# Column-wise softmax sums for the last two head blocks of an attention and gated-MLP kernel, with all final additions on VectorE

## Chip, cores, metric

One core of a Trainium2 chip. The metric is the device time of one execution in microseconds (us). "Span" is the time from the first to the last instruction of one profiled execution; it is about 1.8 us shorter than the device time. Engines are named as the profile names them: PE (TensorE matmul), PEld (TensorE weight load), DVE (VectorE), ACT (ScalarE), POOL (GpSimd), SP (SyncE, which issues the transfers).

## The reference, cut to what matters

```python
B, S, D, H = 1, 2048, 512, 32           # head size 16; MLP width F = 1792; all bf16
xn = layernorm(x)
scores = einsum("bhqd,bhkd->bhqk", q, k) * 16 ** -0.5
p = softmax(scores)                      # 32 x 2048 x 2048 exponentials
out = x + (einsum("bhqk,bhkd->bhqd", p, v) merged) @ wo + mlp(xn)
```

The kernel works on blocks of 512 queries by 4 heads: 32 blocks in all. It multiplies the unnormalised exponentials with V and a column of ones (the "PV" matmuls), so that the softmax sum of each head appears as row 16 of that head's 32 partitions. A block is then divided by its sums, and goes into the output projection.

## The kernel before

The kernel is a list of operations, each with an assumed duration. A static list scheduler in Python simulates the engines with these durations and so fixes the order of the instructions on each engine; each engine then works through its list in that order, waiting on semaphores: in the profile below PE stands 2.65 us at one matmul while others queue behind it.

For 30 of the 32 blocks the division goes through DRAM and POOL, far from the critical path. The last two blocks have no time for this. They spread each sum over its 32 partitions by a matmul with a column of an identity, take the reciprocal of the whole spread tile on DVE, and multiply:

```python
# last-but-one block (one piece of 512 columns); ps_b bank 1 holds the spread sums
def sums(e):
    for j in range(4):                   # 4 heads, 32 partitions each, fp32
        ins = e.matmul(ps_b[32*j:32*j+32, 1, :], ident32[:, 32*j+DH:32*j+DH+1].to_broadcast([128, 32]),
                       o_sb[:, to.slot, :], start=True, stop=True, tile_position=(0, 32*j))
    return ins
G.op("PE", 920, sums, mode="col", ...)
G.op("DVE", 680, lambda e: e.reciprocal(rb[:, tr.slot, :], ps_b[:, 1, :]), ...)     # 680 ns is assumed
G.op("DVE", 610, lambda e: e.tensor_tensor(oT_of(tn), rb[:, tr.slot, :], o_sb[:, to.slot, :], ALU.mult), ...)
# last block: the same in two halves of 256 columns, reciprocal assumed at 400 ns each   [cut]

# final rows: 4 blocks of 128 rows; groups 2, 4, 5 of the projection are still to be added
for i in range(4):
    if i in FIN_PE:                      # FIN_PE = (1,): the residual enters PSUM by 4 fp32 identity matmuls
        for k in range(4):
            G.op("PE", 225, ... e.matmul(bank_of(tz)[:, 128*k:128*k+128], ident32[:], resid(i)[...], start=(k == 0), stop=False) ...)
    for g, pr in ((2, NU-10), (4, NU-9), (5, NU+10)):
        G.op("PE", 216, fn, ...)         # 4 column tiles of the projection; g=4: last-but-one block, g=5: last block
    if i not in FIN_PE:
        G.op("DVE", 610, ... e.tensor_tensor(xn_sb[...], bank_of(tz), resid(i), ALU.add) ...)
    else:
        G.op("ACT", 600, ... e.activation(xn_sb[...], bank_of(tz), ACTF.Copy) ...)
    dma(... out2[128*m:128*(m+1), :] <- xn_sb ...)    # issued by SP, 128 KB
```

Row block 3 collects its projection in `ps_b` bank 1, the same bank that holds the spread sums of the last-but-one block. So its first projection matmul has to wait until the reciprocal has read that bank.

The softmax here doesn't subtract the row's maximum and nothing guards it: scores larger than these inputs give would overflow.

## Time and profile before

| | before |
|---|---|
| device time, three runs | 790.36, 790.53, 791.13 us |
| span of the profiled execution | 788.1 us, mean granted clock 0.996 |
| ACT / PE / DVE busy | 97% / 96% / 94% |
| end of the last exponential | 776.07 us |
| end of the last addition | 784.66 us |
| end of the last output issue | 785.44 us |

The page's first part: busy time of each engine, share of the span, number of instructions.

```profile
PE 756.7 (96%) x9270; PEld 225.2 (29%) x9270; DVE 740.0 (94%) x1065; ACT 763.3 (97%) x679; POOL 165.0 (21%) x178
```

Over most of the span all three of ACT, PE and DVE are nearly full; ACT, with its exponentials, is the fullest. The end differs. First the timeline of ACT: start, duration, line, operation, and in brackets the idle time before it and what ended it.

```profile
734.10 32.90 ACT L1232 ACTIVATE ring<-ps_sc 128x1024 bf16<-128x1024 f32 x29
770.71 5.36 ACT L1232 ACTIVATE ring<-ps_sc 128x1536 bf16<-128x1536 f32 x5 [3.72 <-PE ps_sc L1164]
782.99 0.60 ACT L1274 ACTIVATE xn_sb<-ps_sc 128x512 bf16<-128x512 f32 x1 [6.92 <-PE ps_sc L1262]
```

ACT starves for 3.72 us before its last five exponentials, because PE has made no scores. DVE's timeline of the same stretch:

```profile
764.82 3.35 DVE L1080 RECIPROCAL rb<-ps_b 128x512 f32<-128x512 f32 x1
768.09 1.16 DVE L1197 TENSOR_TENSOR dring<-dring 128x2048 bf16<-128x2048 bf16 x1
769.16 0.68 DVE L1081 TENSOR_TENSOR x_sb<-rb,Wv 128x512 bf16<-128x512 f32 x1
777.19 0.76 DVE L1061 COPY Wv<-ps_b 128x256 f32<-128x256 f32 x2 [7.34 <-PE ps_b L1140]
778.62 1.76 DVE L1042 RECIPROCAL rb<-ps_b 128x256 f32<-128x256 f32 x1 [0.68 <-PE ps_b L1036]
780.30 1.69 DVE L1042 RECIPROCAL rb<-ps_sc 128x256 f32<-128x256 f32 x1
781.91 0.69 DVE L1047 TENSOR_TENSOR x_sb<-rb,Wv 128x256 bf16<-128x256 f32 x2
782.77 1.29 DVE L1271 TENSOR_TENSOR xn_sb<-ps_sc,xnT 128x512 bf16<-128x512 f32 x2 [0.18 <-PE ps_sc L1262]
783.98 0.68 DVE L1271 TENSOR_TENSOR xn_sb<-ps_b,xnT 128x512 bf16<-128x512 f32 x1
```

(The trace names tiles by the memory they reuse: "Wv" is here the evicted PV block, "x_sb" the normalised one, "xnT" the residual.) The scheduler took the first reciprocal for 0.68 us; it takes 3.35. From the waits, in us: total, times, longest:

```profile
ACT ring L1232 <- PE ps_sc L1164: 3.7, 1, 3.7
PE ps_b L1262 <- DVE rb L1080: 2.6, 1, 2.6
```

PE stood 2.6 us at a final-projection matmul (L1262), and the scores for ACT stood in the queue behind it. PE's timeline and the windows view (stretch, length, busy us and instructions of PE, PEld, DVE, ACT and POOL, granted clock, DMA share, GB/s) show what followed:

```profile
768.23 0.62 PE L1262 MATMUL ps_b<-Wo,x_sb 128*32 128x512 bf16 x4 [2.65 <-DVE rb L1080]
```

```profile
765.00:768.00 3.00, 0.58 (x10) 0.09 (x2) 3.00 (x1) 2.00 (x2) 0.00 (x0) 0.99 0.00 0
768.00:771.00 3.00, 2.77 (x27) 0.66 (x27) 1.85 (x3) 0.29 (x1) 0.00 (x0) 0.50 0.00 0
```

After the stall PE ran on half a clock (0.50; in finer windows from 767.9 to 771.3).

### The profile page before, as it was taken

To read this page: it belongs to the slowest core of one execution; us is meant where nothing else is said; L and a number is where in the kernel's file an instruction comes from. 1 tells how busy PE (TensorE), PEld (TensorE's weight loads), DVE (VectorE), ACT (ScalarE), POOL (GpSimd) and SP (SyncE) were. 2 spreads that over 40 slices of the span, in tenths; PEclk is the share of its full clock that TensorE was granted. 3 is DMA by queue.
4 is the path that set the end of the run, shared out by engine and by line. 5 is a ranking of instruction groups with operands and counts; after the bars stand their busy time and mean duration, and the time that the engine had idled before them with its cause. 6 is when DMAs were issued, how large, how long until landed. Compare 5 with 4: busy or idle time off the path is not lost.

```text
span 788.1 us, 21088 instructions
## 1 busy us (share of the span) xinstructions
PE 756.7 (96%) x9270; PEld 225.2 (29%) x9270; DVE 740.0 (94%) x1065; ACT 763.3 (97%) x679; POOL 165.0 (21%) x178
## 2 busy tenths in 40 slices
PE   8999999999999999999999999999999999999986
PEld 4322222222222222222222223222222222223322
DVE  7689999999999899999999999999999899999994
ACT  6999999999999999999999999999999999999992
POOL 4112131221222113122122112212211212212200
PEclk9999999999999999999999999999999999999998
DMA  7312121212221122211221112221222112332000
GB/s 215 108 47 65 41 70 36 63 48 61 56 70 42 36 62 63 68 46 47 72 56 51 42 49 76 51 66 32 73 55 69 35 53 71 71 82 55 29 15 28
DMA packets 95756, 46.82 MB, mean 59 GB/s; under 512 B 69936, under 2 KB 91824, under 8 KB 95664
## 3 DMA queue, kind: packets, MB, share of 16 engines
q1 hardware_dynamic: 95664, 45.46, 21.3%
q8 instruction: 73, 1.20, 0.6%
q14 instruction: 19, 0.16, 0.1%
HBM read 36.70 MB, written 8.50 MB: 57 GB/s over the span
## 4 chain that ended last, share of the span: by engine, by line
DVE 46%; PE 26%; ACT 26%; issue 1%; DVEq 0%
ACT ring L1232 25%; DVE dring L1180 16%; PE ps_b L697 10%; DVE dring L1196 8%; PE ps_sc L1164 7%; DVE dring L1197 6%; PE ps_b L1140 5%; DVE dring L1192 4%; DVE dring L1194 4%; DVE up_sb L916 3%; DVE hT L920 2%; PE ps_b L1164 2%; DVE Wv L1068 1%; PE ps_b L863 1%; DVE xn_sb L958 1%
## 5 line engine op out<-in xcount | busy, mean ns | idle before, releaser
L1232 ACT ACTIVATE ring<-ps_sc 128x1536 bf16<-128x1536 f32 (+1 forms) x663 | 755.2, 1279 | 6.6 <-PE ps_sc L1164 4.9
L1180 DVE TENSOR_SCALAR dring<-ps_b 128x512 uint16<-128x512 f32 x392 | 269.5, 687 | 19.4 <-PE ps_b L1164 18.8
L1164 PE MATMUL ps_sc<-qm,kT 32*128 32x512 bf16 x1656 | 264.7, 385 | 6.6 <-ACT ring L1232 4.1
L1164 PE MATMUL ps_b<-qm,kT 32*128 32x512 bf16 x392 | 150.1, 383 | 8.8 <-DVE dring L1180 6.3
L1140 PE MATMUL ps_b<-ring,v_aug 128*17 128x512 bf16 x1656 | 152.1, 384 | 0.3 <-DVE Wv L1068 0.2
L1094 POOL TENSOR_TENSOR rrec<-rsum,minus 128x16 f32<-128x16 f32 x30 | 96.3, 3211 | 228.6 <-DMA rsum<-Wv 228.6
L1164 PEld LDWEIGHTS ps_sc<-qm,kT 32*128 32x128 bf16 x1656 | 63.4, 91 | 231.5 <-ACT ring L1232 202.3
L1197 DVE TENSOR_TENSOR dring<-dring 128x2048 bf16<-128x2048 bf16 x98 | 119.5, 1219 | 0.0
L1196 DVE TENSOR_TENSOR dring<-dring 128x2048 f16<-128x2048 bf16 x98 | 119.4, 1219 | 0.0
L1104 POOL TENSOR_TENSOR x_sb<-Wv,rb 128x128 bf16<-128x128 f32 x100 | 46.3, 465 | 285.3 <-DVE dring L1197 77.7
L1192 DVE TENSOR_SCALAR dring<-dring 128x2048 uint16<-128x2048 uint16 x98 | 67.9, 693 | 1.7
L697 PE MATMUL ps_b<-xnT,wus 128*32 128x512 bf16 x896 | 67.9, 384 | 1.1 <-DVE hT L920 0.6
L1194 DVE TENSOR_SCALAR dring<-dring 128x2048 uint16<-128x2048 uint16 x98 | 67.6, 689 | 0.0
L697 PE MATMUL ps_b<-xnT,wgs 128*32 128x512 bf16 x896 | 66.2, 383 | 1.3 <-DVE up_sb L916 1.0
L1140 PE MATMUL ps_b<-dring,vd 128*17 128x512 bf16 x784 | 65.5, 381 | 0.0
L697 PE MATMUL ps_b<-Wd,hT 128*32 128x512 bf16 x768 | 59.8, 383 | 0.1
L1140 PEld LDWEIGHTS ps_b<-ring,v_aug 128*17 128x17 bf16 x1656 | 38.5, 89 | 65.3 <-issue 46.7
L1164 PEld LDWEIGHTS ps_b<-qm,kT 32*128 32x128 bf16 x392 | 35.6, 91 | 66.0 <-DVE dring L1180 52.9
L1140 PE MATMUL ps_b<-dring,v_aug 128*17 128x512 bf16 x392 | 38.6, 384 | 1.5 <-DVE dring L1197 0.7
L1282 PE MATMUL ps_b<-zeros 128*17 128x512 bf16 x456 | 38.9, 382 | 0.0
L916 DVE COPY up_sb<-ps_b 128x512 f32<-128x512 f32 x56 | 38.4, 686 | 0.2 <-PE ps_b L697 0.2
L920 DVE SCALAR_TENSOR_TENSOR hT<-ps_b,up_sb 128x512 bf16<-128x512 f32 x48 | 32.9, 686 | 0.9 <-PE ps_b L697 0.9
(105 smaller groups left out, 363.3 us busy)
## 6 DMA issues: line engine op xcount, KB each, us to landing
rb<-rec_scr SPq DMA_DIRECT2D x30, 256.0 KB
wus<-in_B_W_up_dram SPq DMA_DIRECT2D x56, 128.0 KB, 3.5
wgs<-in_B_W_gate_dram SPq DMA_DIRECT2D x56, 128.0 KB, 2.3
qm<-q_scr SPq DMA_DIRECT2D x30, 128.0 KB
o_scr<-x_sb SPq DMA_DIRECT2D x25, 128.0 KB
q_scr<-qT SPq DMA_DIRECT2D x17, 128.0 KB
xr_sb<-in_A_x_dram SPq DMA_DIRECT2D x16, 128.0 KB, 2.5
out_dram<-xn_sb SPq DMA_DIRECT2D x16, 128.0 KB, 1.8
```

What stands on the lines that cost most here:

```text
L697: ins = e.matmul(bank_of(tile, sub)[32 * j:32 * j + 32, :], st[:, 32 * j:32 * j + 32], mv, start=(i == 0), stop=(i == n - 1), tile_positio ...
L916: G.op("DVE", 610, lambda e: e.tensor_copy(up_sb[:, tup.slot, :], bank_of(tu)), reads=[tu], writes=[tup], prio=slots[1] + EV)
L920: G.op("DVE", 610, lambda e: e.scalar_tensor_tensor(out=h_of(th), in0=bank_of(tg), scalar=0.0, in1=up_sb[:, tup.slot, :], op0=ALU.max, op1 ...
L1094: G.op("POOL", 3000, lambda e: e.tensor_tensor(rrec[:, par, :], rsum[:, par, :], minus[:, 0:1].to_broadcast([128, 16]), ALU.pow), reads=[t ...
L1140: ins = e.matmul(ps_b[32 * j:32 * j + VN, 0, :], v, src[j][1](k), start=(first and k == 0), stop=(last and (k == 2 or not on)), tile_posit ...
L1164: return e.matmul(bank, kT[32 * j:32 * j + 32, gg, 128 * kt:128 * kt + 128], qm[32 * j:32 * j + 32, t_q[(c4, gg)].slot, ee, :], start=True ...
L1180: o = G.op("DVE", 610, lambda e, j=j: e.tensor_scalar(dring[:, tr.slot, 0, 512 * j:512 * j + 512].bitcast(U16), ps_b[:, 2, :], 0.25 * LOG2 ...
L1192: G.op("DVE", 600, lambda e: e.tensor_scalar(b(2, U16), b(0, U16), 0x7F, 0x3F80, op0=ALU.bitwise_and, op1=ALU.bitwise_or), reads=[tr], wri ...
L1194: G.op("DVE", 600, lambda e: e.tensor_scalar(b(1, U16), b(0, U16), 0xFF80, N_MANT, op0=ALU.bitwise_and, op1=ALU.bitwise_or), reads=[tr], w ...
L1196: G.op("DVE", 1140, lambda e: e.tensor_tensor(b(2, FP16), b(2), b(2), ALU.mult), reads=[tm], writes=[tm], prio=u - 3, name="d4", lock=True)
L1197: G.op("DVE", 1140, lambda e: e.tensor_tensor(b(2), b(0), b(2, FP16), ALU.mult), reads=[tm, tr], writes=[tm], prio=u - 3, name="d5", lock= ...
L1232: return e.activation(ring[:, a:a + n, :], ps_sc[:, 3 * k0:3 * k0 + n, :], ACTF.Exp, scale=0.25)
```

## The change

The intent: a reciprocal costs by the column (3.35 us for 512 columns, 1.69 to 1.76 for 256). The sums are only 4 x 512 numbers, so bring them into 16 columns by 128 partitions, invert those, and spread the result afterwards, again with PE. The block is used as the stationary operand and four columns of the identity as the moving one: this transposes just the sum rows. The spread multiplies a broadcast column with the whole identity. Two details come along: row block 1's addition moves from PE and ACT to DVE (`FIN_PE` empty), and the PV matmuls of the last 14 units rather than 5 get early priority. The identity additions' own priority is changed too, which does nothing while `FIN_PE` is empty but matters in e6. The diff is cut; lines after "..." are paraphrased.

```diff
-FIN_PE = (1,)
+FIN_PE = ()
+PV_LAST = 14
+        def spread_sums(src, c0, c1, par, bank_s, bank_r, rd, t_s, t_r, pr, opens=None):
+            def sums(e):
+                for c in range(c0, c1):
+                    ins = e.matmul(bank_s(4 * c, 4 * c + 4), src(128 * c, 128 * c + 128), ident32[:, DH:128:32], start=True, stop=True)
+                return ins
+            o = G.op("PE", 240 * (c1 - c0), sums, mode="full", ...)
+            G.op("DVE", 180, lambda e: e.reciprocal(rrec2[:, par, 4 * c0:4 * c1], bank_s(4 * c0, 4 * c1)), ...)
+            def spread(e):
+                for c in range(c0, c1):
+                    for j in range(4):
+                        ins = e.matmul(bank_r(32 * j, 128 * c), rrec2[:, par, 4 * c + j:4 * c + j + 1].to_broadcast([128, 32]), ident32[:],
+                                       start=True, stop=True, tile_position=(0, 32 * j))
+                return ins
+            G.op("PE", 270 * (c1 - c0), spread, mode="col", ...)
 ... last block, each half h:
-   sums (460) / reciprocal 128x256 (400) / multiply
+   spread_sums(src, 2 * h, 2 * h + 2, ...)
+   t_fin[h].w.append(G.op("DVE", 350, ... ps * src -> oT ...))     # reads the spread from PSUM
 ... last-but-one block:
-   sums (920) / reciprocal 128x512 (680) / multiply
+   spread_sums(lambda a, b: o_sb[:, to.slot, a:b], 0, 4, 0, ..., pr + 80)
+   G.op("DVE", 610, lambda e: e.tensor_tensor(oT_of(tn), ps_b[:, 1, :], o_sb[:, to.slot, :], ALU.mult), ...)
-   prio=u + PV_LAG - (200 if u > NU - 5 else 0)
+   prio=u + PV_LAG - (200 if u > NU - PV_LAST else 0)
 ... identity additions of FIN_PE (row blocks 0 to 2):
-   prio=NU + 2
+   prio=NU - 190
```

More of the change, by code (lines that the diff above doesn't have):

```diff
@@ L483, in bass_parallel_sum__mha_block__glu_gated_reglu__prompt_kernel @@
         rb = sb("rb", [128, 2, 512], FP32)
+        rrec2 = sb("rrec2", [128, 2, 16], FP32)
         rsum = sb("rsum", [128, 2, 16], FP32)
@@ L1021, in bass_parallel_sum__mha_block__glu_gated_reglu__prompt_kernel @@
         t_half, t_fin = [Tile(), Tile()], [Tile(), Tile()]
+        def spread_sums(src, c0, c1, par, bank_s, bank_r, rd, t_s, t_r, pr, opens=None):
+            def sums(e):
+                ins = None
+                for c in range(c0, c1):
+                    ins = e.matmul(bank_s(4 * c, 4 * c + 4), src(128 * c, 128 * c + 128), ident32[:, DH:128:32], start=True, stop=True)
+                return ins
+            o = G.op("PE", 240 * (c1 - c0), sums, mode="full", reads=[rd, t_id32], writes=[t_s], prio=pr - 100, name="sum")
+            if opens is not None:
+                o.opens = ("tail", [o])
+            t_rec = Tile()
+            G.op("DVE", 180, lambda e: e.reciprocal(rrec2[:, par, 4 * c0:4 * c1], bank_s(4 * c0, 4 * c1)), reads=[t_s], writes=[t_rec], prio=pr - 900, name="rec")
+            def spread(e):
+                ins = None
+                for c in range(c0, c1):
[3 more added lines that the diff above has]
+                return ins
+            G.op("PE", 270 * (c1 - c0), spread, mode="col", reads=[t_rec, t_id32], writes=[t_r], prio=pr - 100, name="spread")
+            if opens is not None:
+                G.ops[-1].opens = ()
         def last_normalise(to, pr):
@@ L1025, in src @@
                 return o_sb[:, to.slot, a:b]
-            tn, tr = Tile("oT", P_oT), Tile("rb", P_rb)
-            tt = [Tile("ls", P_b, [2]), Tile("lb", P_sc, [1])]
+            tn = Tile("oT", P_oT)
+            ts = [Tile("ls", P_b, [2]), Tile("lb", P_sc, [1])]
             for h in range(2):
-                def bank(h=h):
-                    return ps_b[:, 2, 256 * h:256 * h + 256] if h == 0 else ps_sc[:, 3, 256 * h:256 * h + 256]
-                def sums(e, h=h, bank=bank):
-                    ins = None
-                    for j in range(4):
-                        ins = e.matmul(bank()[32 * j:32 * j + 32, :], ident32[:, 32 * j + DH:32 * j + DH + 1].to_broadcast([128, 32]),
-                                       src(256 * h, 256 * h + 256), start=True, stop=True, tile_position=(0, 32 * j))
-                    return ins
-                o = G.op("PE", 460, sums, mode="col", reads=[t_half[h], t_id32], writes=[tt[h]], prio=pr - 100, name="sum")
-                o.opens = ("tail", [o]) if h == 0 else ()
-                t_rec = Tile()
-                G.op("DVE", 400, lambda e, h=h, bank=bank: e.reciprocal(rb[:, tr.slot, 256 * h:256 * h + 256], bank()), reads=[tt[h]], writes=[t_rec] + ([tr] if h == 0 else []),
-                     prio=pr - 900, name="rec")
@@ L1044, in last_normalise @@
+                t_r = Tile("lr")
+                spread_sums(src, 2 * h, 2 * h + 2, 1, lambda a, b, h=h: (ps_b[:, 2, :] if h == 0 else ps_sc[:, 3, :])[:, a:b],
+                            lambda p, c, h=h: ps_sc[p:p + 32, 4, c:c + 128] if h else ps_b[p:p + 32, 2, c:c + 128],
+                            t_half[h], ts[h], ts[h] if h == 0 else t_r, pr, opens=True if h == 0 else None)
                 if h:
-                    tr.w.append(G.ops[-1])
-                    G.ops[-1].order.add(tr.w[0])
@@ L1047, in last_normalise @@
-                t_fin[h].w.append(G.op("DVE", 330, lambda e, h=h: e.tensor_tensor(oT_of(tn)[:, 256 * h:256 * h + 256], rb[:, tr.slot, 256 * h:256 * h + 256], src(256 * h, 256 * h + 256), ALU.mult),
-                     reads=[t_rec, t_half[h]], writes=[tn] if h == 0 else [], prio=pr - 900, lock=True))
+                    ts[1].w.append(G.ops[-1])
+                t_fin[h].w.append(G.op("DVE", 350, lambda e, h=h: e.tensor_tensor(oT_of(tn)[:, 256 * h:256 * h + 256],
+                                                                              (ps_sc[:, 4, 256:512] if h else ps_b[:, 2, 0:256]), src(256 * h, 256 * h + 256), ALU.mult),
+                     reads=[ts[h], t_half[h]] + ([t_r] if h else []), writes=[tn] if h == 0 else [], prio=pr - 900))
@@ L1070, in normalise @@
             if (c4, gg, ee) == (NB - 1, NGG - 1, 0):
-                tn, tr, ts, t_rec = Tile("oT", P_oT), Tile("rb", P_rb), Tile("ls", P_b, [1]), Tile()
-                def sums(e):
-                    ins = None
-                    for j in range(4):
-                        ins = e.matmul(ps_b[32 * j:32 * j + 32, 1, :], ident32[:, 32 * j + DH:32 * j + DH + 1].to_broadcast([128, 32]),
-                                       o_sb[:, to.slot, :], start=True, stop=True, tile_position=(0, 32 * j))
-                    return ins
-                G.op("PE", 920, sums, mode="col", reads=[to, t_id32], writes=[ts], prio=pr - 20, name="sum")
-                G.op("DVE", 680, lambda e: e.reciprocal(rb[:, tr.slot, :], ps_b[:, 1, :]), reads=[ts], writes=[tr], prio=pr - 900, name="rec")
-                G.op("DVE", 610, lambda e: e.tensor_tensor(oT_of(tn), rb[:, tr.slot, :], o_sb[:, to.slot, :], ALU.mult),
-                     reads=[tr, to], writes=[tn], prio=pr - 900, lock=True)
+                tn, ts, tr = Tile("oT", P_oT), Tile("ls", P_b, [1]), Tile("lr", P_b, [1])
+                spread_sums(lambda a, b: o_sb[:, to.slot, a:b], 0, 4, 0, lambda a, b: ps_b[:, 1, a:b], lambda p, c: ps_b[p:p + 32, 1, c:c + 128], to, ts, tr, pr + 80)
+                G.op("DVE", 610, lambda e: e.tensor_tensor(oT_of(tn), ps_b[:, 1, :], o_sb[:, to.slot, :], ALU.mult),
+                     reads=[tr, to], writes=[tn], prio=pr - 900)
                 t_oT[(c4, NGG + ee)] = tn
@@ L1142, in pv @@
                     return ins
-                G.op("PE", 225, pv, mode="col", reads=rd, writes=[pv_tile[key]], prio=u + PV_LAG - (200 if u > NU - 5 else 0), name="pv%d" % u,
+                G.op("PE", 225, pv, mode="col", reads=rd, writes=[pv_tile[key]], prio=u + PV_LAG - (200 if u > NU - PV_LAST else 0), name="pv%d" % u,
                      after=u + PV_MIN)
@@ L1254, in bass_parallel_sum__mha_block__glu_gated_reglu__prompt_kernel @@
                     G.op("PE", 225, lambda e, i=i, tz=tz, k=k: e.matmul(bank_of(tz)[:, 128 * k:128 * k + 128], ident32[:], resid(i)[:, 128 * k:128 * k + 128], start=(k == 0), stop=False),
-                         mode="full", reads=[t_id32, t_res[m]], writes=[tz], prio=NU - 20 if i == 3 else NU + 2)
+                         mode="full", reads=[t_id32, t_res[m]], writes=[tz], prio=NU - 20 if i == 3 else NU - 190)
             for g, pr in ((2, NU - 10), (4, NU - 9), (5, NU + 10)):
```

## The prediction

> **What bounds the kernel now.** Over most of the span ScalarE: the page gives ACT 97% busy (exponentials), PE 96%, DVE 94%. The change touches only the last 25 us of 788.1, where two stretches of DVE reciprocal bound it (timeline and chain of waits):
> 1. The last-but-one head pair's RECIPROCAL, 128x512, 3.35 us from 764.82. PE, in order, stands 2.65 us behind it at a final-projection matmul that needs the same bank; no scores are made and ACT sits idle 3.72 us before 770.71. The windows view shows granted clock 0.50 for 768.2 to 770.7. The Trainium skill (TensorE: Matmul & The Clock Gate, Part 1) says that an idle PE is returned to half clock; this trace agrees.
> 2. In the tail, two RECIPROCALs of 128x256 (1.76 and 1.69 us) stand back to back between the sums and the last multiplications. From the end of the last exponential (776.07) to the end of the last addition (784.66) is 8.6 us.
>
> **Cost of the parts.** (3.35-1.72)/256 gives 6.4 ns per column of a reciprocal and about 0.1 us fixed. The Trainium skill (VectorE: DVE Perf Modes, the 8-slice pipeline) speaks of an iterated divide with repeat count 8; the trace shows about 6 cycles at 0.96 GHz, dear by the column anyway. Estimates from it: 16 columns 0.2 us, 8 columns 0.15. So 6.8 us of DVE become about 0.5.
> Added on PE: sums as columns need a full fp32 128x128 weight load each. The identity additions (same stationary size, 128 columns moving) step at 0.42 us; with four moving columns I estimate 0.22, so 0.9 us for the first pair and 0.45 per half. The spread resembles the old sums (512 columns 1.07 us, 256 about 0.6): 1.0 and 0.5 us. Multiplications stay 0.68 and 0.38 us.
> Removed on PE: four identity additions, 1.7 us from 775.6 to 779.3, two ahead of the last PV and one ahead of the last sums (about 0.7 us on the chain). Moved: row block 1's addition from ACT (0.60, parallel) to DVE (0.62 more on the chain).
>
> **On the critical path.** First stretch: the wait for the bank shrinks to what the scheduler assumed, PE doesn't stall or cool, ACT runs on: I expect 3.1 to 3.6 of the 3.72 us idle to go, and the last exponential to end near 772.7. Earlier PV (last 14 units) is worth little by itself.
> Tail, from the last exponential: PV 0.6, eviction 0.45, sums 0.65, reciprocal 0.2, spread 0.65, multiplication 0.4, projection 0.45, four additions 2.5: about 6.0 us against 8.6. Gain 2.3 to 2.6.
> Together 5.4 to 6.2 us of 790.5, 0.7%.
>
> **Predicted:** 784.7 us, 8 in 10 within 782.8 to 787.2. Faster by over 2%: 0.01; within 2%: 0.985; slower by over 2%: 0.005.
>
> **What would show it.** Timeline: RECIPROCALs of 128x16 and twice 128x8, each under 0.25 us; ACT's idle before its last five exponentials under 0.6 us; granted clock near 1.0 up to the last exponential, which ends 772.3 to 773.3; no identity matmuls; four DVE additions in a row, ending about 6 us after it; nothing changed before about 750 us.
>
> **What would make it wrong.** Full-array fp32 sums or 16 small spread matmuls at 2x the estimate, on a PE nearly full there (the chain runs through PE from 740 to 761), so ACT still starves 1 to 2 us; early PV pushing back the last output job, which frees the bank that the sums need; projection matmuls landing between sums and spread in PE's order; a changed order of earlier work; the clock dropping in PE gaps of the tail.

## More of the kernel before

SP's timeline shows the four output issues back to back, 1.95 us, up to 785.44:

```profile
783.49 1.95 SPq L1276 DMA_DIRECT2D out_dram<-xn_sb  x4
```

## The result

The changed kernel took 783.2, 783.4 and 784.0 us, the kernel before in the same rounds 790.21 to 791.13: ratio 0.9911, 95% interval 0.9892 to 0.9931. A ratio here is the mean time of one kernel's fast runs over that of the other's in the same rounds, so not quite the ratio of the medians that are quoted. One more execution, the first and the only profiled one, took 1069.93 us with a granted clock of 0.556 from start to end: a slow state of the chip. It is left aside; none of the later executions of this kernel or its variants showed it, and why that one did is open. The kernel was therefore run once more, unaltered, as the first experiment (783.24 to 783.54 us, five runs; ratio 0.9907, interval 0.9888 to 0.9925). The lines below are from that run.

The page's first part of the kernel after:

```profile
PE 754.2 (97%) x9306; PEld 226.4 (29%) x9306; DVE 734.8 (94%) x1066; ACT 762.5 (98%) x678; POOL 165.7 (21%) x178
```

ACT's timeline now ends with one row of 34 exponentials without a gap, up to 734.29 + 38.06 = 772.35 us, 3.72 us earlier than before:

```profile
734.29 38.06 ACT L1240 ACTIVATE ring<-ps_sc 128x1024 bf16<-128x1024 f32 x34
```

DVE's timeline (all three reciprocals are now L1036):

```profile
764.43 0.25 DVE L1036 RECIPROCAL rrec<-ps_b 128x16 f32<-128x16 f32 x1
764.60 1.16 DVE L1204 TENSOR_TENSOR dring<-dring 128x2048 f16<-128x2048 bf16 x1
772.91 0.76 DVE L1077 COPY Wv<-ps_b 128x256 f32<-128x256 f32 x2 [5.29 <-PE ps_b L1148]
774.03 0.21 DVE L1036 RECIPROCAL rrec<-ps_b 128x8 f32<-128x8 f32 x1 [0.37 <-PE ps_b L1030]
774.48 0.21 DVE L1036 RECIPROCAL rrec<-ps_sc 128x8 f32<-128x8 f32 x1 [0.24 <-PE ps_sc L1030]
775.08 0.42 DVE L1062 TENSOR_TENSOR x_sb<-ps_b,Wv 128x256 bf16<-128x256 f32 x1 [0.40 <-PE ps_b L1042]
776.01 1.89 DVE L1279 TENSOR_TENSOR xn_sb<-ps_sc,xnT 128x512 bf16<-128x512 f32 x3
777.82 0.68 DVE L1279 TENSOR_TENSOR xn_sb<-ps_b,xnT 128x512 bf16<-128x512 f32 x1
```

6.8 us of reciprocal have become 0.67. What PE pays (L1030 are the column sums, L1042 is here the spread) is near the estimates; its timeline for the last-but-one block and for the first half of the last:

```profile
762.64 1.05 PE L1030 MATMUL ps_b<-ident,Wv 128*128 128x4 f32 x8
764.73 1.08 PE L1042 MATMUL ps_b<-ident,rrec 128*32 128x128 f32 x32
773.39 0.61 PE L1030 MATMUL ps_b<-ident,Wv 128*128 128x4 f32 x4
774.37 0.64 PE L1042 MATMUL ps_b<-ident,rrec 128*32 128x128 f32 x16
```

The windows view: no stall, and the clock stays at 1.00.

```profile
765.00:768.00 3.00, 2.93 (x59) 1.12 (x51) 2.58 (x3) 3.00 (x4) 0.00 (x0) 1.00 0.00 0
768.00:771.00 3.00, 3.00 (x45) 0.87 (x45) 0.00 (x0) 3.00 (x4) 0.00 (x0) 1.00 0.00 0
```

SP's timeline: the last output issue ends at 776.73 + 2.12 = 778.85 us.

```profile
776.73 2.12 SPq L1284 DMA_DIRECT2D out_dram<-xn_sb  x4
```

A comparison of the instruction orders in the two traces shows them identical on all engines up to about 760 us. So all that differs lies at the end, and the span can be cut into three pieces: up to the end of the last exponential; from there to the end of the last output issue; and the rest, which is 2.6 to 2.7 us in every one of these profiles (before: 788.1 - 785.44; after: 781.5 - 778.85) and so tells nothing. The two first pieces, from the ACT and SP timelines:

| kernel (profiled run) | last exponential ends | from there to end of last issue | span | clock |
|---|---|---|---|---|
| before | 776.07 | 9.37 | 788.1 | 0.996 |
| after (e0) | 772.35 | 6.50 | 781.5 | 0.999 |
| e1: only the last-but-one block changed | 772.41 | 9.05 | 784.1 | 0.998 |
| e2: only the last block changed | 775.09 | 7.19 | 784.9 | 1.000 |
| e3: only FIN_PE and PV priority | 776.55 | 9.01 | 788.2 | 0.994 |
| e4: before, true durations for the scheduler | 772.27 | 9.60 | 784.5 | 0.997 |
| e5: e1 with a useless wide reciprocal | 776.90 | 9.14 | 788.7 | 0.994 |
| e6: after, FIN_PE back | 772.48 | 6.97 | 782.1 | 1.000 |
| e7: after, PV priority back | 772.87 | 6.66 | 782.2 | 0.999 |
| e8: after, two residuals by bf16 matmul | 772.10 | 6.57 | 781.3 | 1.000 |
| e9: e2 with true duration | 772.09 | 7.42 | 782.2 | 1.000 |
| e10: e8 with two output transfers | 772.36 | 5.75 | 780.8 | 0.999 |
| e11: e8, last transfer issued by ACT | 772.56 | 6.11 | 781.4 | 0.999 |

The gain of 6.6 us of span is 3.7 us of ACT's stall and 2.9 us of tail.

### The profile page after: what moved, and what is told of

It reads as the page before. It is cut to its first block, busy times and chain, and to the rows that moved or that the text cites. A ratio compares the mean times of both kernels' runs of the same rounds, so it can differ in the third digit from the quotient of the medians.

```text
span 1068.1 us, 21160 instructions
## 1 busy us (share of the span) xinstructions
PE 1060.4 (99%) x9306; PEld 249.2 (23%) x9306; DVE 766.3 (72%) x1066; ACT 797.9 (75%) x678; POOL 161.9 (15%) x178
## 4 chain that ended last, share of the span: by engine, by line
PE 98%; DVE 1%; ACT 1%; issue 0%; DVEq 0%
PE ps_b L699 34%; PE ps_b L1148 26%; PE ps_sc L1172 24%; PE ps_b L1172 8%; PE ps_b L1290 4%; PE ps_b L865 1%; ACT ring L1240 0%; PE ps_b L648 0%; PE ps_sc L1270 0%; PE ps_b L1042 0%; PE ps_b L1030 0%; DVE dring L1188 0%; PE ps_sc L648 0%; DVE Wv L1084 0%; PE ps_sc L711 0%
## 5 line engine op out<-in xcount | busy, mean ns | idle before, releaser
L1240 ACT ACTIVATE ring<-ps_sc 128x1536 bf16<-128x1536 f32 (+1 forms) x663 | 789.6, 1235 | 245.9 <-PE ps_sc L1172 146.3
L1172 PE MATMUL ps_sc<-qm,kT 32*128 32x512 bf16 x1656 | 337.8, 481 | 1.1 <-ACT ring L1240 0.6
L1148 PE MATMUL ps_b<-ring,v_aug 128*17 128x512 bf16 x1656 | 211.6, 530 | 0.2
L1172 PE MATMUL ps_b<-qm,kT 32*128 32x512 bf16 x392 | 195.3, 498 | 1.0 <-DVE dring L1188 1.0
L699 PE MATMUL ps_b<-xnT,wus 128*32 128x512 bf16 x896 | 99.3, 543 | 0.1
L699 PE MATMUL ps_b<-xnT,wgs 128*32 128x512 bf16 x896 | 98.3, 550 | 0.1
L1148 PE MATMUL ps_b<-dring,vd 128*17 128x512 bf16 x784 | 97.3, 551 | 0.0
L699 PE MATMUL ps_b<-Wd,hT 128*32 128x512 bf16 x768 | 88.6, 549 | 0.0
L1290 PE MATMUL ps_b<-zeros 128*17 128x512 bf16 x444 | 54.3, 534 | 0.0
L1148 PE MATMUL ps_b<-dring,v_aug 128*17 128x512 bf16 x392 | 53.5, 534 | 0.0
```

Source lines behind the costliest of these rows:

```text
L699: ins = e.matmul(bank_of(tile, sub)[32 * j:32 * j + 32, :], st[:, 32 * j:32 * j + 32], mv, start=(i == 0), stop=(i == n - 1), tile_positio ...
L1148: ins = e.matmul(ps_b[32 * j:32 * j + VN, 0, :], v, src[j][1](k), start=(first and k == 0), stop=(last and (k == 2 or not on)), tile_posit ...
L1172: return e.matmul(bank, kT[32 * j:32 * j + 32, gg, 128 * kt:128 * kt + 128], qm[32 * j:32 * j + 32, t_q[(c4, gg)].slot, ee, :], start=True ...
L1240: return e.activation(ring[:, a:a + n, :], ps_sc[:, 3 * k0:3 * k0 + n, :], ACTF.Exp, scale=0.25)
L1290: ins = e.matmul(ps_b[32 * j:32 * j + VN, 0, :], zeros[:, 0:VN], zmov, start=False, stop=False, tile_position=(0, 32 * j))
```

## The experiments

**Theory:** (1) the 3.35 us reciprocal of the last-but-one block cost time only because PE, in order, stood behind it and starved ACT; (2) the two halves of the last reciprocal lay on the chain of the tail. **Rivals:** the order of PE's work (PV priority, FIN_PE) made the gain; or all of it is in the tail; or DVE's time is itself what counts in the first part, so that only a short reciprocal helps.

Each kernel ran in five rounds (four to six runs) beside the kernel before; e0 to e3, e4 to e7, e8 and e9, e10 and e11 were sent together, each set to one chip but not all to the same one, so medians of different sets are compared with care. All were correct.

### e0: the changed kernel again

> The changed kernel unaltered, once more, because its profiled execution fell in a slow state (clock 0.56 from start to end). Expected in a fast state: 783.0 to 784.3 us, 6.5 to 7.3 us under the kernel before. Theory (stall gone plus shorter tail): ACT's idle before its last five exponentials under 0.6 us, last exponential ends 772.3 to 773.3, last addition 5.5 to 6.2 us after it. Rival (gain is all in the tail): ACT still idles over 2 us there.

783.3 us median, 7.5 under the 790.85 of its rounds, a shade more than the 6.5 to 7.3 expected. ACT's stall is wholly gone, the last exponential ends at 772.35 and the last addition 6.15 us later (778.50). The theory's figures for the trace hold; the rival that expected ACT to idle still falls.

### e1: only the last-but-one block

```diff
 kernel before, with
+ spread_sums(...) for block (3, 3, 0)      # last_normalise, FIN_PE, PV priority as before
```

> The kernel before with only the last-but-one head pair changed (column sums, 16-column reciprocal, spread). Theory: this alone removes the ACT idle of 3.72 us, so 3.2 to 3.9 us faster than before, i.e. about 787.0. Rival 1 (the tail is where all of the gain lies, and the stall is hidden): within 1 us of before. Rival 2 (the order of PE work, PV_LAST, is needed for it): under 2 us gain.

786.13 us median, ratio 0.9943 (0.9928 to 0.9958): 4.5 us faster than before, somewhat above the range of 3.2 to 3.9 set for it. ACT's idle is 0.21 us, and the last exponential ends at 772.41:

```profile
764.05 8.36 ACT L1249 ACTIVATE ring<-ps_sc 128x1024 bf16<-128x1024 f32 x8 [0.21 <-PE ps_sc L1181]
```

The rivals fall: this part alone, without any change of priority, removes the stall.

### e2: only the last block

```diff
 kernel before, with
+ last_normalise of the changed kernel      # last-but-one block, FIN_PE, PV priority as before
```

> The kernel before with only the last head pair changed. Theory: the tail loses two reciprocals of 1.7 us and gains two spreads and fuller sums, 2.4 to 3.2 us faster than before (about 787.7), and the early ACT idle of 3.7 us stays. Rival (the tail hides behind other work): within 1 us of before.

788.34 us median, ratio 0.9966 (0.9948 to 0.9983): 2.7 us faster. The tail is 2.2 us shorter (7.19 against 9.37), and the stall stays, as expected. But its six runs fall into two sorts: 786.72 and 786.94 at a mean clock of 1.000, and 788.0 to 788.99 at 0.996 to 0.997. The profiled run was of the first sort. Its PE, ACT and windows lines:

```profile
768.56 0.40 PE L1277 MATMUL ps_b<-Wo,x_sb 128*32 128x512 bf16 x4 [2.64 <-DVE rb L1095]
```

```profile
769.97 5.12 ACT L1247 ACTIVATE ring<-ps_sc 128x1536 bf16<-128x1536 f32 x5 [2.65 <-PE ps_sc L1179]
```

```profile
768.00:771.00 3.00, 2.44 (x37) 0.79 (x41) 2.17 (x3) 1.03 (x1) 0.00 (x0) 1.00 0.00 0
```

PE stood just as long as in the kernel before (2.64 us against 2.65), in the same order of instructions, but here the clock stayed at 1.00 and ACT lost 2.65 us instead of 3.72. So the 3.72 us are 2.65 of waiting and 1.07 of half clock after it: from the end of its wait to the end of the next scores PE needs 2.44 us in the kernel before and 1.36 here. The same order of instructions and the same stall can go either way. Two more profiled stalls, 2.56 us in e3 and 2.83 us in e5, were followed by half clock too, each time for about 3.4 us; in e3 it set in 0.75 us after PE had resumed. So of four stalls of nearly one length three were followed by it. The Trainium skill (TensorE: Matmul & The Clock Gate, Part 1) says that the activity window runs freely and isn't tied to the kernel's start; two outcomes of one stall agree with that.

The spread of the kernel before fits it: of its 11 runs in these rounds, the three at a mean clock of 0.996 or more took 789.06 to 789.13 us, the eight at 0.992 to 0.994 took 790.17 to 792.58, while the changed kernel, which has no stall, spread over 0.3 us in e0. But the mean doesn't show which outcome a run had. It also counts the half clock after the last matmul (from 785.0 to the end in the profile before), and that profiled run, with half clock after its stall, has a mean of 0.996 and took 789.88 us. Whether the slower runs of e2 and of the kernel before had half clock after the stall is therefore likely and not shown; no trace of them was kept.

### e3: only the priorities

```diff
-FIN_PE = (1,)
+FIN_PE = ()
-... (200 if u > NU - 5 else 0)
+... (200 if u > NU - 14 else 0)
```

> The kernel before with only FIN_PE empty and the PV priority over the last 14 units. Theory: no more than 0.7 us either way, because both reciprocals stay: identity additions off the chain give 0.5 to 0.7 us, the fourth addition on DVE takes 0.6 back. Rival (most of the gain is the reordering): 3 us or more faster.

789.8 us median, ratio 0.9984 (0.9968 to 1.0001): 1.3 us, more than the 0.7 expected, but with an interval that reaches 1. ACT still stalls, in two pieces (2.21 and 1.34 us). The rival "it is the reordering" falls.

### e4: the kernel before with true durations

```diff
-G.op("DVE", 680, lambda e: e.reciprocal(rb[:, tr.slot, :], ...        # last-but-one block
+G.op("DVE", 3280, lambda e: e.reciprocal(rb[:, tr.slot, :], ...
-G.op("DVE", 400, ... e.reciprocal(rb[:, tr.slot, 256*h:256*h+256], ... # last block
+G.op("DVE", 1650, ...
```

> The kernel before with nothing changed but the two durations that its static scheduler assumes for the wide reciprocals (680 to 3280 ns and 400 to 1650 ns, as the trace measures them); the instructions are the same, only PE's order moves. Theory (the 3.7 us of ACT idle came from PE's in-order queue standing at a matmul that waits for the bank): PE now does PV and scores before that matmul, ACT's idle there drops under 1 us, the clock stays near 1.0, 2.5 to 4 us faster than before, about 787. Rival (3.35 us of DVE is itself on the chain, so only a shorter reciprocal helps): within 1 us of before.

786.73 us median, ratio 0.9955 (0.9943 to 0.9968): 3.6 us faster than before. On ACT and DVE the traces show the same instructions in the same order as before; PE's order differs from 765.7 us on. The wide reciprocal is still there, 3.35 us long, and ACT runs through it without a gap:

```profile
765.04 3.35 DVE L1080 RECIPROCAL rb<-ps_b 128x512 f32<-128x512 f32 x1
```

```profile
734.32 37.95 ACT L1232 ACTIVATE ring<-ps_sc 128x1024 bf16<-128x1024 f32 x34
```

The last exponential ends at 772.27, as in the changed kernel. The scheduler, told the truth, put the waiting projection matmul behind PV and two more rounds of scores, and PE waits 0.16 us at it:

```profile
767.67 0.61 PE L1282 MATMUL ps_b<-zeros 128*17 128x512 bf16 x8
768.45 0.40 PE L1262 MATMUL ps_b<-Wo,x_sb 128*32 128x512 bf16 x4 [0.16 <-DVE rb L1080]
```

The first of these lines is a thing not mentioned so far: where the scheduler expects PE to be too idle, it puts in blank matmuls, products with zeros. It placed two groups of four here, and in all one group fewer than before (452 of these matmuls against 456), so the list of instructions isn't quite the same. In the 2.65 us gap of the kernel before there is none. The blanks are not needed for the gain: e1 and the changed kernel have none after 690 us. So DVE's 3.35 us were never on the chain by themselves: the rival falls, and part (1) of the theory is shown.

### e5: a useless wide reciprocal put back

```diff
 e1, with, in front of the 16-column reciprocal
+    e.reciprocal(up_sb[:, 0, :], ps_b[:, 1, :])     # 128x512, result unused; assumed duration unchanged
```

> The version with only the last-but-one pair changed, with a useless 128x512 reciprocal put back on DVE right before the 16-column one; PE's order is the same as in that version. Theory (length of the DVE instruction in front of an in-order PE): PE stalls at the spread for about 3 us and ACT starves again by 2.5 to 4 us, so the gain of 4.5 us mostly goes, 789 to 791 us. Rival (the form of the sums or the bank use made the gain): stays within 1 us of 786.1.

791.17 us median (789 to 791 expected), ratio 1.001 (0.9997 to 1.0022): the whole gain of e1 is gone, and the profile's waits show the stall again, now at the spread (L1044), with ACT's as its consequence:

```profile
ACT ring L1252 <- PE ps_b L1160: 3.6, 1, 3.6
PE ps_b L1044 <- DVE rrec L1037: 2.8, 1, 2.8
```

PE's order is the same as in e1, matmul by matmul in the traces. So neither the form of the sums nor the bank made the gain: an unforeseen 3.35 us in front of an in-order PE makes or unmakes it.

### e6 and e7: one detail of the change undone

```diff
 e6: changed kernel, FIN_PE = (1,)
 e7: changed kernel, PV_LAST = 5
```

> The changed kernel with one part undone: row block 1's residual again added by four identity matmuls on PE and copied out by ACT. Theory: the four matmuls (0.42 us each) land before the last PV and put it back 0.5 to 0.9 us, one addition fewer on DVE gives 0.6 back: within 0.5 us of the changed kernel. Rival (four additions in a row on DVE are what bounds the end): 0.5 us or more faster than the changed kernel.

> The changed kernel with one part undone: early PV only for the last 5 units instead of 14. Theory: within 0.4 us of the changed kernel (783.3). Rival (the earlier PV keeps ACT fed): slower by 1 us or more, with ACT idle in the last 20 us.

e6 took 784.02 us median (ratio 0.9922, 0.991 to 0.9934), e7 783.84 (0.9918, 0.9905 to 0.9932), against 783.3 (0.9907) for the changed kernel in an earlier set of rounds; the intervals overlap, so by the medians the details are worth 0.7 and 0.5 us, a little more than the 0.5 and 0.4 allowed for, and the intervals don't make it sure. The rival of e7 (1 us or more) falls: its last exponential ends 0.52 us later, after 0.22 us of ACT idle at 764.5, and its tail is 0.16 us longer. In e6 the tail is 0.47 us longer, and PE's timeline shows three identity additions ahead of the last PV but one, and one more ahead of the last:

```profile
771.51 0.94 PE L1262 MATMUL ps_sc<-xnT,ident 128*128 128x128 f32 x6
772.38 0.39 PE L1148 MATMUL ps_b<-ring,v_aug 128*17 128x512 bf16 x4
772.70 0.49 PE L1262 MATMUL ps_sc<-xnT,ident 128*128 128x128 f32 x2
773.12 0.39 PE L1148 MATMUL ps_b<-ring,v_aug 128*17 128x512 bf16 x4
```

The last PV starts at 773.12 rather than 772.46. This isn't quite the order of the kernel before, which has two of the four ahead of its last PV: the changed kernel gives them a higher priority (NU - 190 rather than NU + 2), so e6 doesn't undo that one detail alone. From the start of the last PV to the last addition e6 takes 5.54 us against 6.04, so one addition fewer on DVE did give back 0.5 us there; but the last issue ends 6.33 us after it against 6.39, so nearly nothing was left, which the expectation (0.6 us) and its rival both missed. That pointed to another bound on the end.

### e8: two of four additions off DVE

```diff
 changed kernel, with FIN_B = (1, 3):
-            return xnT[:, i, 0:1024].bitcast(FP32)
+            return xnT[:, i, 0:512] if i in FIN_B else xnT[:, i, 0:1024].bitcast(FP32)   # residual kept in bf16
+                if g == 4 and i in FIN_B:                      # one bf16 identity matmul, 128x512
+                    G.op("PE", 225, ... e.matmul(bank_of(tz), ident[:], resid(i), start=False, stop=False) ...)
 blocks 1 and 3 are copied out by ACT
```

> A version meant to beat both: the changed kernel, with the residuals of row blocks 1 and 3 kept as bf16 and added by one bf16 identity matmul each (128x512), so that ACT copies out two of the four blocks beside DVE's two additions. Theory (four additions of 0.62 us in a row on DVE bound the end): last piece ready about 1.0 us earlier, 782.2 to 782.8 us, 0.6 to 1.1 us under the changed kernel. Rival (output issue and landing bound the end, not the additions): within 0.3 us of the changed kernel.

783.52 us median, ratio 0.9918 (0.9904 to 0.9931): no gain. The additions did get done sooner (DVE and ACT both end by 777.30, against 778.50), and yet SP's last issue ends at 776.72 + 1.95 = 778.67:

```profile
776.71 0.59 ACT L1286 ACTIVATE xn_sb<-ps_b 128x512 bf16<-128x512 f32 x1
776.72 1.95 SPq L1288 DMA_DIRECT2D out_dram<-xn_sb  x4
```

My theory of the end falls: SP needs 1.95 us for four issues in a row (344 to 599 ns each), and it can't start before the first block is ready at about 776.7. When the additions are faster, the issues queue; when they are slower, as in the changed kernel, each issue (332 to 400 ns) hides behind the next addition.

### e9: the first part of the change replaced by a true duration

```diff
 e2, with
-G.op("DVE", 680, lambda e: e.reciprocal(rb[:, tr.slot, :], ...
+G.op("DVE", 3280, lambda e: e.reciprocal(rb[:, tr.slot, :], ...
```

> Only the last pair changed, and the last-but-one pair's wide reciprocal kept but told to the scheduler at its true 3280 ns. Theory (the first part of the change is worth only what PE's order is worth): no ACT idle, 783.6 to 784.8 us, within 1.3 us of the changed kernel. Rival (the short first reciprocal has a worth of its own): 786 us or more.

784.37 us median, ratio 0.9928 (0.9915 to 0.994). ACT runs without a gap to 772.09. So the short reciprocal of the last-but-one block buys nothing that a correct number in the schedule would not; what is left to the changed kernel (about 1.1 us by the medians) lies in the tail (7.42 against 6.50), where the identity additions still stand in this version. No run has the wide reciprocal with its true duration and all else as in the changed kernel, so what the identity additions cost there isn't measured alone.

### e10 and e11: fewer issues in SP's row

```diff
 e10: e8, output blocks (0,1) and (2,3) as two transfers of 256 KB
 e11: e8, block 3's transfer issued by ACT after its own copy
```

> The version with two bf16 identity additions (783.5 us), with its four output transfers of 128 KB made two of 256 KB (blocks 0 and 1, blocks 2 and 3). Theory (SyncE's row of four issues of 0.34 to 0.6 us each bounds the end, since the last data were ready at 777.3 but the last issue ended at 778.67): last issue ends at about 777.85, a gain of 0.3 to 0.8 us over that version, 782.7 to 783.2 us. Rival (the 512 KB themselves take that long to move): within 0.2 us of it.

> The same version, with the last output transfer (block 3) issued by ScalarE itself right after it has written the block; SyncE issues the other three. Theory (SyncE's row of issues): last issue ends near 778.05 instead of 778.67, a gain of 0.3 to 0.7 us, 782.8 to 783.2 us. Rival (moving the data bounds the end): within 0.2 us.

e10: 782.5 us median (782.34 to 783.13; 782.7 to 783.2 expected), ratio 0.9905 (0.9892 to 0.9919); two issues take 0.95 us, and the tail is 5.75 us against e8's 6.57:

```profile
777.16 0.95 SPq L1292 DMA_DIRECT2D out_dram<-xn_sb  x2
```

e11: 783.2 us median, ratio 0.9913 (0.9899 to 0.9926), tail 6.11 us. Both tails are shorter though the same bytes move, and the rest of the span, in which the data land, is hardly longer (2.69 and 2.73 us against 2.63); so SP's row of issues was what stood there, and the rival (moving the data) falls. e11's time is not clearly better than e8's: its tail is 0.46 us shorter, but its last exponential ended 0.46 us later, so its last issue ends at 778.67 as in e8, and the medians differ by 0.3 us. e10 has the lowest median of all versions, 0.8 us under the changed kernel, but it wasn't timed in the same rounds as it and the ratios' intervals overlap, so that it beats it is likely and not shown. The Trainium skill (DMA: Bandwidth & Descriptors, "Issuing engines are not separate DMA queues") says that a second issuing engine saves only the issue time, which it calls usually small relative to the transfer itself. A single issue agrees (0.34 to 0.60 us against 1.8 us to landing); but here, at the very end, the four stand in a row and take 1.95 us.

## Why the prediction was right

The predicted 784.7 us (782.8 to 787.2) met medians of 783.4 (fast runs) and 783.3 (e0), and its two mechanisms are the ones shown.

- *ACT's stall.* It was to lose 3.1 to 3.6 of its 3.72 us; it lost all. e1, e4 and e5 show that cause: PE's in-order wait behind a reciprocal whose length the scheduler did not know.
- *The half clock.* Read rightly from the windows view, but put down to the stall as if it always came. e2 shows that the same stall can pass without it; it makes 1.07 of the 3.72 us in the profiled one.
- *Costs of the parts.* Reciprocals 0.25 and twice 0.21 us (0.2 and 0.15 estimated; 0.251 just misses "under 0.25"), column sums 1.05 us (0.9) and 0.61 (0.45 per half; the second half starts 0.46 after the first), spread 1.08 (1.0) and 0.64 (0.5).
- *The tail.* Last exponential to last addition: 6.15 us measured, 6.0 predicted. Each of its terms was within 0.15 us.
- *The mis-sized terms.* "Row block 1's addition from ACT (0.60, parallel) to DVE (0.62 more on the chain)" was wrong in what it costs. The chain does not end at the last addition but at the last output issue; in the kernel before, where ACT took one addition, the issues queued behind the data (last addition 784.66, last issue 785.44), while after, the last issue ends 0.35 us behind its addition. So 0.43 of the 0.62 us came back, (785.44 - 784.66) - (778.85 - 778.50). The second mis-sized term is the stall, 0.37 us above the middle of its range. Together 0.8 of the 1.4 us between 784.7 and 783.3; the other 0.65 is the starting point: the profiled execution before took 789.88 us, and the prediction subtracted what it read there from the median of 790.53. e6 and e8 show the same from the other side: fewer additions on DVE gave next to nothing at the last issue.
- *The reference time.* 790.5 us was itself likely a mixture of outcomes of the clock; in these rounds the kernel before ranged over 3.5 us, more than the width of some of the effects.

The change was built for shorter reciprocals. Of its 6.6 us of span, the 3.7 us before the last exponential could have been had by correcting one assumed duration (e4, e9); only the tail, 2.9 us, needed other instructions: about 2 us of it is the last block's narrow reciprocals (9.37 to 7.19 in e2, to 7.42 in e9).

## What to carry to other kernels

When an in-order engine starves another, compare the measured duration of the instruction it waits for with the one that the schedule assumed, before making that instruction faster: a wrong 0.68 for 3.35 us was worth 3.6 us here. Follow the end of a kernel to the last transfer's issue, not to the last arithmetic, and count issues there. When a kernel's runs spread, look at the granted clock around each stall and not only at its mean: a stall that is followed by half clock in some executions only makes the time, and any gain over it, vary.

## What the Trainium skill lacked or had wrong

- VectorE: DVE Perf Modes speaks of a repeat count of 8 for the reciprocal, without a time. Measured here for fp32: 128x512 3.35 us, 128x256 1.69 to 1.76, 128x16 0.19 (e5) to 0.25, 128x8 0.21; between the wide ones 6.2 to 6.5 ns per column, about 6 cycles at 0.96 GHz. If a repeat took one cycle it would be 8; the page doesn't say that it does.
- TensorE: Matmul & The Clock Gate advises against PE gaps over about 3 us. Gaps of 2.65 us (the kernel before), 2.56 (e3) and 2.83 (e5) were followed by half clock in the profiles, and a gap of 2.64 us in the same order of instructions as the first was not (e2). The advice is too generous by some tenths, and gaps of this length have this cost in some executions and not in others.
- The same page's rule for a weight load, columns over 1.2 GHz, gives 107 ns for 128 columns. The fp32 loads of 128x128 took 186 to 192 ns, and each fp32 matmul appears as two loads and two matmuls in the trace (four column-sum matmuls as 8 records); that page gives no fp32 times; other pages speak of fp32 passes, and none gives a time for such a load.
- DMA: Bandwidth & Descriptors gives about 50 ns of dispatch for transfers issued from GpSimd and no measured time for an issue on SyncE; for that it has only a count of sequencer cycles for "previous generations", in its section on trn3 B0. Measured on SyncE here: 332 to 400 ns when spaced by other work, 344 to 599 ns in a row of four; 256 KB issued as fast (395 to 464 ns) as 128 KB.
